# New numbers for the whole work order of a fused attention and feed-forward kernel, with a constant and a copy moved from VectorE to ScalarE

## The chip, the cores and the metric

The kernel runs on one core of a Trainium2 chip. Its engines are TensorE (PE in the profile, PEld for its weight loads), VectorE (DVE), ScalarE (ACT), GpSimd (POOL) and SyncE (SP), which here only issues DMAs. Each engine takes its own instructions strictly in the order in which they were built, and waits at the head of its queue for what other engines owe it. The metric is the device time of one execution in microseconds. Three executions took 1113.07, 1113.84 and 1115.66 us; the median is 1113.84 us. The profile is of one further execution, which took 1110.31 us and whose span from the first to the last instruction is 1108.5 us.

## The reference

Kernelised attention with random features, and behind it a feed-forward network with GELU:

```
scale = 1 / sqrt(sqrt(64));  q, k = q * scale, k * scale
phi(x) = exp(h - max(h)) / sqrt(128),  h = x @ omega.T - sum(x*x)/2
kv  = sum over s of phi(k)[s] outer v[s];   z = sum over s of phi(k)[s]
out = (phi(q) @ kv) / (phi(q) @ z + 1e-6)
x   = out, heads side by side              # 4608 tokens x 512
y   = gelu(x @ w_in) @ w_out               # w_in 512 x 2048, w_out 2048 x 512
```

There are 8 batches and 8 heads of 576 tokens with 64 dimensions, and 128 features.

## The kernel before

The attention is cut into 32 **units**, each with two heads of one batch. The first four (batch 0) are worked on in a plain form before the feed-forward starts; the next four (batch 1, `mode == 1`) in a middle form; the 24 units of batches 2 to 7 (`mode == 2`) in an exact split form, which is most of the work. The feed-forward runs over 12 **blocks** of 384 tokens. A block has 16 **chunks** of 128 hidden columns: `mm1` (L706, 12 matmuls of 384 columns), GELU and its two halves on ACT (L718, L719) and DVE (L724), and two chunks later `mm2` (L740 to L742, 9 matmuls of 512 columns). Block 0 is computed in fp32 (L693, L736), the other eleven in split fp16.

A unit of the third form goes through these steps:

- `x_high`, `x_low` (ACT L286, POOL L292): a slice of k or q is copied rounded and its rest subtracted, into one of three buffers `r`. `proj` (PE L299, 5 groups) and `proj_q` (PE L327, 4 groups) project it; `proj_lo` and `proj_add` (ACT L304, DVE L310, L311) take k's results, `q_blocks` (DVE L335, L337) q's. `k_shift` (POOL L316) subtracts k's maxima.
- `q_max` to `q_shift`: the maximum of q over all features. PE turns the partial maxima (L343), DVE reduces and spreads them (L347, L349), PE turns them back (L353), ACT copies (L356), DVE adds them to q's half of the tile `et` (L362). Then `exps` (ACT L370) takes all of `et`.
- `k_high`, `k_low`, `kv` (POOL L423, DVE L431, PE L450), five groups: the products with v. `kv_a` to `kv_d` (ACT L459, DVE L466 to L468, ACT L474, DVE L478) bring the sums into `kvh` and `kvl`: the numerators' columns, and beside them the denominator's column spread to 64 columns.
- `q_back`, `q_high`, `q_low`: q's exponentials in their layout.
- `num`, `den`, `div`, once for each half of the tokens: six matmuls (PE L518); two copies of the denominators (ACT L527, L528) into `dt`; then DVE turns `dt` (L535), adds the constant (L536), takes the reciprocal (L537), turns it back (L538) and multiplies (L546, L547) into `xs`, the input of a block. For the first two forms `den` is one copy (L525).

At the start of a block `block_max` (DVE L658), a short chain over PE, DVE and POOL (L192 to L215, L670 to L672), `block_high` and `block_low` (ACT L679, DVE L684) make the block's scales and its split input.

All results of PE's attention steps go into one ring of three PSUM banks, named `at`: a step that needs a bank waits until the step that had it has been read.

What sets the order is a list of **events**. Each step is entered with a number, its slot: `at(t, step, ...)`. The events are sorted by slot and the instructions are recorded in that sequence. A chunk takes 6 slots, a block 96; a third-form unit stands at a burst `t` (every 33.4 slots for the first eight, then every 36), its steps at fixed distances from `t`. The slots are no times: they only decide which instruction stands before which.

Of the kernel before, what the change touches and what calls it, by code (L numbers as in the profile page):

```python
# [19 lines left out]
P = 128  # L20
# [5 lines left out]
TOP = 13  # L26


@with_exitstack
def favor_attention_ffn(ctx: ExitStack, tc: tile.TileContext, qT, kT, v, omT, w_in, w_out, out):  # L30
# [430 lines left out]
    def kv_b(u):  # L461
# [6 lines left out]
        nc.vector.tensor_copy(kz[:, 1:3], kvs[:, :, D:D + 1].broadcast_to([P, 2, D]))  # L468
# [52 lines left out]
    def den(u, half):  # L521
        pe, po = u.pn[half]
        u.dt = sp.tile([P, HS], F32, tag="dt", name="dt", bufs=1)
        if u.mode < 2:
            nc.scalar.copy(u.dt, po[:, 0:HS])  # L525
            return
        nc.scalar.copy(u.dt[0:D], pe[D:P, 0:HS])  # L527
        nc.scalar.copy(u.dt[D:P], po[0:D, 0:HS])  # L528

    def div(u, half):  # L530
# [5 lines left out]
        nc.vector.tensor_scalar(rc, rv[:, :, 0], EPS * (1.0 if u.mode < 2 else KSC), None, op0=ALU.add)  # L536
        nc.vector.reciprocal(rc, rc)  # L537
# [232 lines left out]
    for i, u in enumerate(units[:NJ]):  # L770
        t = BASE + 9 * i
        at(t - 4, load_plain, u)
        for g in range(3):
            at(t + 2 * g, proj_plain, u, g)
        at(t + 6, kv_plain, u, ps_any)
        at(t + 7.3, kvz_plain, u, ps_any)
        for g in range(3):
            at(t + 7 + g, q_trans, u, g, ps_any)
            at(t + 7.5 + g, q_copy, u, g)
        for half in range(2):  # L780
            at(t + 11.2 + half, num, u, half, ps_any)
            at(t + 11.3 + half, den, u, half)
            at(t + 11.4 + half, div, u, half)

    at(BASE - 3, nc.vector.memset, ones, 1.0)
    for i in range(NF):
        pi, po = piece(True, i), piece(False, i)
        w_events(pi, BASE + 1 + 5 * i if i < WEARLY else SUB * i - 27, (-6, 0, 1, 2, 3))
        w_events(po, 5.5 * i, (-7, 0, 1, 2, 3))
        for pc, t in ((pi, 72 + 4.5 * i), (po, 91 + 4.5 * i)):  # L790
            at(t, w_high, pc)
            at(t + 1, w_low, pc)
    for win, t in ((1, 68), (0, 86.5)):
# [4 lines left out]
    bursts = [5 + 20.5 * k for k in range(NJ)]  # L798
    bursts += [112 + 33.4 * k if k < 8 else 346 + 36 * (k - 7) for k in range(len(units) - 2 * NJ)]
    load_at = -40  # L800
    for k, u in enumerate(units[NJ:]):
# [3 lines left out]
        if u.mode == 1:  # L805
            first = t - 13 + 3 * (k == 0)
            for i in range(3):
                at(first + (0, 6, 7.5)[i], proj_mid, u, i)
            load_at = first + 7.7
            at(t + 5.5, kv_plain, u, ps_at)  # L810
            at(t + 8, kvz_plain, u, ps_at)
            for g in range(3):
                at(t + 9 + 2 * g, q_trans, u, g)
                at(t + 9.6 + 2 * g, q_copy, u, g)
        else:
            pk, pq = [t - 27 + 1.75 * i for i in range(NK)], [t - 16 + 2 * i for i in range(4)]
            load_at = pq[-1] - 1.8
# [110 lines left out]
```

## Time and profile before

| | |
|---|---|
| median of three runs | 1113.84 us |
| profiled execution, its span | 1110.31 us, 1108.5 us |
| mean granted clock of TensorE | 0.988 |
| third-form units, exponentials (ACT L370) | from 205 us to 946 us |

The span falls into four stretches: up to about 55 us the plain units and the loads; up to 205 us the first block in fp32, the middle units and the conversion of the weights; up to 942 us the 24 third-form units beside the fp16 blocks; and after that feed-forward alone. A row of a waits view reads: engine, tile and line that waited, the releaser, the time in total, how often, and the longest.

### The profile page before, as it was taken

The numbers are of one execution on the slowest core, as the hardware profiler recorded it, in microseconds if no ns is written. First come the engines' busy times: TensorE is split into PE (matmuls) and PEld (weight loads), VectorE is DVE, ScalarE is ACT, GpSimd is POOL, SyncE is SP. The second block draws the span as 40 slices with busy tenths as digits, with TensorE's granted clock in tenths as the row PEclk, the third lists the DMA queues.
The fourth block names the chain that finished last, engine by engine and source line by source line (L and its number), as shares of the span: only waits on it lengthen the run. The fifth ranks groups of instructions, "written<-read, shape, count | busy, mean of one in ns | idle before, by whom it ended". The sixth has DMA issues, their size and how long they took to land.

```text
span 1108.5 us, 17209 instructions
## 1 busy us (share of the span) xinstructions
PE 1031.4 (93%) x5949; PEld 604.4 (55%) x5949; DVE 829.7 (75%) x1888; ACT 650.4 (59%) x1298; POOL 472.7 (43%) x606
## 2 busy tenths in 40 slices
PE   8988898999899999989799999989889999999998
PEld 6654454555455555555455555555555555555555
DVE  6989759988988888887887887997687798631312
ACT  7866454656566766656466666656656656533332
POOL 2224336545566644545654445655434555100000
PEclk9999999999999999999999999999999999999999
DMA  8565421211222112122221122222112220000000
GB/s 233 168 184 168 125 55 34 72 35 54 84 55 55 48 58 55 46 73 55 56 73 45 33 74 55 56 83 56 34 51 55 56 84 1 1 29 1 29 1 29
DMA packets 46279, 70.91 MB, mean 64 GB/s; under 512 B 13680, under 2 KB 22256, under 8 KB 46192
## 3 DMA queue, kind: packets, MB, share of 16 engines
q1 hardware_dynamic: 46192, 69.81, 22.1%
q8 instruction: 47, 0.77, 0.3%
q14 instruction: 40, 0.33, 0.1%
HBM read 60.36 MB, written 9.44 MB: 63 GB/s over the span
## 4 chain that ended last, share of the span: by engine, by line
PE 40%; DVE 31%; ACT 8%; issue 4%; POOL 4%; DMA 1%; POOLq 0%; DVEq 0%; ACTq 0%
PE h L706 17%; PE acc L742 5%; PE acc L741 5%; PE acc L740 5%; DVE gl L724 5%; DVE et L335 3%; DVE mx L337 2%; DVE ql L386 2%; DVE kl L431 2%; ACT gh L719 2%; ACT et L370 2%; DVE wil L170 1%; DVE rt L535 1%; PE at L450 1%; ACT g L718 1%
## 5 line engine op out<-in xcount | busy, mean ns | idle before, releaser
L706 PE MATMUL h<-xl,wih 128*128 128x384 f16 x704 | 230.8, 328 | 0.0
L706 PE MATMUL h<-xh,wih 128*128 128x384 f16 x704 | 230.7, 328 | 0.0
L706 PE MATMUL h<-xh,wil 128*128 128x384 f16 x704 | 230.3, 327 | 0.0
L724 DVE SCALAR_TENSOR_TENSOR gl<-g,bs,gh 128x384 f16<-128x384 f32 x176 | 127.2, 729 | 129.3 <-ACT gh L719 128.7
L292 POOL TENSOR_TENSOR r<-xt,r 64x256 fp32r<-64x256 f32 (+2 forms) x216 | 170.4, 798 | 105.3 <-ACT r L286 83.7
L740 PE MATMUL acc<-woh,gh 128*128 128x512 f16 x528 | 200.2, 379 | 1.8 <-DVE o L753 1.8
L741 PE MATMUL acc<-woh,gl 128*128 128x512 f16 x528 | 199.1, 377 | 0.0
L742 PE MATMUL acc<-wol,gh 128*128 128x512 f16 x528 | 199.0, 377 | 0.0
L718 ACT ACTIVATE g<-h,bs 128x384 f32<-128x384 f32 x176 | 101.7, 579 | 153.9 <-PE h L706 152.7
L706 PEld LDWEIGHTS <-wih 128*128 128x128 f16 x1408 | 134.3, 98 | 83.5 <-issue 0.6
L423 POOL TENSOR_SCALAR kh<-et 128x256 f16<-128x256 f32 (+1 forms) x120 | 50.8, 429 | 224.1 <-ACT et L370 141.3
L286 ACT CAST r<-xt 128x256 fp32r<-128x256 f32 (+2 forms) x216 | 87.4, 406 | 80.1 <-PE at L327 70.1
L719 ACT ACTIVATE gh<-g,bs 128x384 f16<-128x384 f32 x176 | 106.6, 614 | 2.8
L706 PEld LDWEIGHTS <-wil 128*128 128x128 f16 x704 | 69.1, 98 | 42.6 <-issue 0.7
L742 PEld LDWEIGHTS <-gh 128*128 128x128 f16 x544 | 53.4, 98 | 59.1 <-issue 0.8
L150 POOL TENSOR_TENSOR w<-w,raw 128x512 int32<-128x512 int32 x32 | 42.4, 1328 | 90.1 <-DVE w L146 52.5
L740 PEld LDWEIGHTS <-gh 128*128 128x128 f16 x544 | 53.2, 98 | 41.8 <-issue 0.6
L741 PEld LDWEIGHTS <-gl 128*128 128x128 f16 x544 | 53.5, 98 | 37.6 <-issue 2.6
L327 PE MATMUL at<-r,om 128*128 128x288 f32 x192 | 55.0, 368 | 20.4 <-DVE rc L537 10.0
L377 DVE STREAM_TRANSPOSE qt<-et 128x288 f32<-128x288 f32 x96 | 43.8, 465 | 37.1 <-ACT et L370 36.9
L299 PE MATMUL at<-om,r 128*128 128x256 f32 x216 | 63.6, 366 | 7.8 <-DVE kvz L467 7.7
L431 DVE SCALAR_TENSOR_TENSOR kl<-et,kh 128x256 f16<-128x256 f32 (+1 forms) x120 | 54.3, 465 | 15.6 <-POOL kh L423 14.5
(174 smaller groups left out, 2022.1 us busy)
## 6 DMA issues: line engine op xcount, KB each, us to landing
xt<-in_kT SPq DMA_DIRECT2D x56, 288.0 KB, 3.8
xt<-in_qT SPq DMA_DIRECT2D x56, 288.0 KB, 3.8
v<-in_v SPq DMA_DIRECT2D x32, 320.0 KB, 3.2
out_x<-o SPq DMA_DIRECT2D x35, 256.0 KB, 2.0
raw<-in_w_in SPq DMA_DIRECT2D x16, 512.0 KB, 4.5
raw<-in_w_out SPq DMA_DIRECT2D x16, 512.0 KB, 3.7
out_x<-o SPq DMA_DIRECT2D x2, 128.0 KB, 1.7
om<-in_omT SPq DMA_DIRECT2D x2, 32.0 KB, 2.2
```

The source lines that it names most:

```text
L286: nc.scalar.copy(u.r[i][:, 0:b - a], xf[:, a:b])
L292: nc.gpsimd.tensor_tensor(r, xf[D:, a:b], r, op=ALU.subtract)
L299: nc.tensor.matmul(u.pp[i][:, t], r[:, t * P:(t + 1) * P], om, start=True, stop=True)
L327: nc.tensor.matmul(ps[:, 0:HS], om[:, i], r, start=(i == 0), stop=(i == 1))
L431: nc.vector.scalar_tensor_tensor(kl[:, :n], es, KSC, kh[:, :n], op0=ALU.mult, op1=ALU.subtract)
L706: nc.tensor.matmul(h[:, 0:T], w, (xh, xh, xl)[k], start=(i == 0), stop=(i == 3 * NJ - 1))
L718: nc.scalar.activation(g, h[:, 0:T], AF.Gelu, scale=bsc[n][1][:, 3:4])
L719: nc.scalar.activation(gh, g, AF.Copy, scale=bsc[n][1][:, 4:5])
L724: nc.vector.scalar_tensor_tensor(gl, g, bsc[n][1][:, 4:5], gh, op0=ALU.mult, op1=ALU.subtract)
L740: nc.tensor.matmul(acc, gh[:, s], woh[:, c, c0:c1], start=(c == 0), stop=False)
L741: nc.tensor.matmul(acc, gl[:, s], woh[:, c, c0:c1], start=False, stop=False)
L742: nc.tensor.matmul(acc, gh[:, s], wol[:, c, c0:c1], start=False, stop=(c == NF - 1))
```

## The change

Three edits of the computation, and new numbers for the order. `kv_b`'s last instruction, the copy that spreads the denominator's column, goes from DVE to ACT. `den`'s copies become activations of the kind Copy that add the constant as a bias. `div` no longer adds it, and takes the reciprocal straight from the turned tile.

```
-        nc.vector.tensor_copy(kz[:, 1:3], kvs[:, :, D:D + 1].broadcast_to([P, 2, D]))
+        nc.scalar.copy(kz[:, 1:3], kvs[:, :, D:D + 1].broadcast_to([P, 2, D]))
...
-            nc.scalar.copy(u.dt, po[:, 0:HS])
+            nc.scalar.activation(u.dt, po[:, 0:HS], AF.Copy, bias=EPS)
...
-        nc.scalar.copy(u.dt[0:D], pe[D:P, 0:HS])
-        nc.scalar.copy(u.dt[D:P], po[0:D, 0:HS])
+        nc.scalar.activation(u.dt[0:D], pe[D:P, 0:HS], AF.Copy, bias=EPS * KSC)
+        nc.scalar.activation(u.dt[D:P], po[0:D, 0:HS], AF.Copy, bias=EPS * KSC)
...
-        nc.vector.tensor_scalar(rc, rv[:, :, 0], EPS * (1.0 if u.mode < 2 else KSC), None, op0=ALU.add)
-        nc.vector.reciprocal(rc, rc)
+        nc.vector.reciprocal(rc, rv[:, :, 0])
```

The slots come from a table `X`; of its some 70 numbers these belong to the steps that the prediction speaks of:

```
-            pk, pq = [t - 27 + 1.75 * i for i in range(NK)], [t - 16 + 2 * i for i in range(4)]
+            pk, pq = [t + X['pk'] + X['dk'] * i for i in range(NK)], [t + X['pq'] + X['dq'] * i for i in range(4)]
...
-            for d, f in ((1.5, q_max), (2, q_max2), (2.5, q_max3), (3, q_max4), (3.5, q_shift)):
-                at(pq[-1] + d, f, u)
+            for d, f in enumerate((q_max, q_max2, q_max3, q_max4, q_shift)):
+                at(pq[-1] + X['qm'] + X['dqm'] * d, f, u)
```

with `pk` -27, `dk` 1.68, `pq` -16, `dq` 2.67, `qm` 3.26, `dqm` 0.12. The products with v start at `t` + 2.57 instead of `t` + 4, the second half's numerators 4.27 slots behind the first's instead of 5. Bursts go from 112 + 33.4 per unit to 110.11 + 34.16, and from the eighth on they stand 3.2 slots later than before, 36 apart as before.

What this does to the queues is shown at three places of one unit, the one whose exponentials start at 780.07 us in the profile. In the changed file every line up to `div` stands 9 further down and those behind it 8 (L335 becomes L344, L724 becomes L732).

DVE in the first half's `div`, from the turn of `dt` on, before:

```order
L535 STREAM_TRANSPOSE rt<-dt 128x288
L536 TENSOR_SCALAR rc<-rt 128x9
L537 RECIPROCAL rc<-rc 128x9
L538 STREAM_TRANSPOSE rt<-rc 128x288
L335 STREAM_TRANSPOSE et<-at 128x288
L546 TENSOR_TENSOR xs_1_8787<-at,rt 64x288
L547 TENSOR_TENSOR xs_1_8787<-at,rt 64x288
```

and in the change:

```order
L544 STREAM_TRANSPOSE rt<-dt 128x288
L545 RECIPROCAL rc<-rt 128x9
L546 STREAM_TRANSPOSE rt<-rc 128x288
L554 TENSOR_TENSOR xs_1_8748<-at,rt 64x288
L555 TENSOR_TENSOR xs_1_8748<-at,rt 64x288
L344 STREAM_TRANSPOSE et<-at 128x288
```

The addition is gone, and the turn of a `q_blocks` has moved from inside the division to behind it.

DVE around the maximum of q, before: the second half's division, the last `q_blocks` (L335, L337) and `q_max2` (L347, L349) stand mixed.

```order
L335 STREAM_TRANSPOSE et<-at 128x288
L538 STREAM_TRANSPOSE rt<-rc 128x288
L337 TENSOR_REDUCE mx<-et 128x9
L546 TENSOR_TENSOR xs_1_8787<-at,rt 64x96
L547 TENSOR_TENSOR xs_1_8787<-at,rt 64x96
L546 TENSOR_TENSOR xs_1_8866<-at,rt 64x192
L547 TENSOR_TENSOR xs_1_8866<-at,rt 64x192
L347 TENSOR_REDUCE sm<-at 36x32
L658 TENSOR_REDUCE xm<-xs_1_8787 128x1
L349 COPY sm<-sm 36x96
L724 SCALAR_TENSOR_TENSOR gl<-g,bs,gh 128x384
L362 TENSOR_TENSOR et<-et,nq 128x1152
```

In the change the division is finished ahead of these rows:

```order
L344 STREAM_TRANSPOSE et<-at 128x288
L732 SCALAR_TENSOR_TENSOR gl<-g,bs,gh 128x384
L346 TENSOR_REDUCE mx<-et 128x9
L356 TENSOR_REDUCE sm<-at 36x32
L358 COPY sm<-sm 36x96
L732 SCALAR_TENSOR_TENSOR gl<-g,bs,gh 128x384
L371 TENSOR_TENSOR et<-et,nq 128x1152
```

The four multiplications and the block's maximum no longer stand between the last partial maximum and `q_max2`'s two instructions.

POOL at the products with v (`kh` is k's high part, `r` the next unit's slices, `vb` and `v` the parts of v), before:

```order
L423 TENSOR_SCALAR kh<-et 128x256 x4
L292 TENSOR_TENSOR r<-xt,r 64x256
L386 TENSOR_TENSOR ql<-qt,qh 128x288
L423 TENSOR_SCALAR kh<-et 128x128
L393 TENSOR_SCALAR vb<-v 128x10x64
```

and in the change:

```order
L432 TENSOR_SCALAR kh<-et 128x256 x4
L432 TENSOR_SCALAR kh<-et 128x128
L301 TENSOR_TENSOR r<-xt,r 64x256
L395 TENSOR_TENSOR ql<-qt,qh 128x288
L301 TENSOR_TENSOR r<-xt,r 64x128
L402 TENSOR_SCALAR vb<-v 128x10x64
```

All five high parts now stand in a row; the next unit's slice and `ql` come behind them.

On PE the same matmuls are issued, 5520 in the program in both. Between the last `proj_q` and `q_max` there stood 8 matmuls of `mm1` in this unit (1.3 us at 0.1625 us each); now 12 and the three of one `mm2` group stand there. Between `q_max` and `q_max3` stood 4 of `mm1` and 5 of `mm2`; now it is 3 of `mm2`.

102 lines of the change are left out of this document (55 added, 47 removed).

## The prediction

> **What bounds the kernel now.** I read the page's head and its chain of work that ended last, then the busy time by stretch, then PE's waits in the stretches where PE idles.
>
> ```profile
> PE 1031.4 (93%) x5949; PEld 604.4 (55%) x5949; DVE 829.7 (75%) x1888; ACT 650.4 (59%) x1298; POOL 472.7 (43%) x606
> ...
> PE 40%; DVE 31%; ACT 8%; issue 4%; POOL 4%; DMA 1%; POOLq 0%; DVEq 0%; ACTq 0%
> ```
>
> PE is the fullest engine, yet only 40% of the chain that ended last is its own work and 31% is DVE's: PE's in-order queue often stands at an instruction for which DVE is late. So the gain to be had is PE's idle time, and a row of work taken from another engine counts only where PE waits for it. Where does PE idle? The two stretches in the middle, with the busy time of PE, PEld, DVE, ACT and POOL:
>
> ```profile
> 55.00:205.00 150.00, 133.45 (x597) 72.22 (x598) 120.38 (x243) 80.73 (x135) 64.21 (x67) 0.95 0.38 109
> 205.00:942.00 737.00, 686.29 (x4028) 403.95 (x4027) 616.24 (x1431) 467.97 (x943) 388.53 (x505) 0.99 0.20 56
> ```
>
> PE idles 737.0 - 686.3 = 50.7 us from 205 to 942 us, the stretch of the 24 third-form units, and 16.6 us from 55 to 205 us. Ahead of them the loads, behind them feed-forward alone leave little to move. What ended PE's idle time from 205 to 942 us:
>
> ```profile
> PE at L327 <- DVE rc L537: 10.0, 4, 4.2
> PE at L299 <- DVE kvz L467: 7.7, 6, 1.9
> PE at L327 <- DVE et L335: 5.6, 12, 0.5
> PE at L450 <- DVE kl L431: 5.5, 15, 1.4
> PE at L518 <- DVE kvl L478: 3.2, 4, 1.4
> PE at L343 <- DVE mx L337: 2.5, 5, 1.0
> PE at L518 <- DVE xs L546: 2.3, 2, 1.2
> PE at L327 <- DVE et L310: 2.2, 3, 0.9
> PE acc L740 <- DVE o L753: 1.8, 1, 1.8
> PE at L518 <- ACT kvh L474: 1.8, 3, 0.9
> PE at L327 <- DVE mx L337: 1.5, 2, 1.0
> PE at L353 <- DVE sm L349: 1.5, 7, 0.2
> PE at L203 <- DVE ct L200: 1.1, 2, 0.5
> ```
>
> These thirteen rows hold 46.7 of the 50.7 us. No single step is to blame: `proj_q` (L327) has 19.3 us, `num` (L518) 7.3 us in these rows, `proj` (L299) 7.7 us, `kv` (L450) 5.5 us. Idle time understates a wait, because a matmul's row reaches over the start of the next one:
>
> ```profile
> L706 PE MATMUL h<-xh,wih 128*128 128x384 f16 x704 | 230.7, 328 | 0.0
> 748.41 1.95 PE h L706 x12
> ```
>
> One row is 328 ns long, but in the chain twelve start within 1.95 us, one in 162.5 ns. So each gap that shows hides about 0.165 us more.
>
> **The three small edits.** Their rows, the DVE instructions that go and the ACT copies that change:
>
> ```profile
> L536 DVE TENSOR_SCALAR rc<-rt 128x9 f32<-128x9 f32 x64 | 22.5, 351 | 0.9
> L468 DVE COPY kvz<-kvs 128x128 f32<-128x128 f32 x24 | 7.0, 293 | 0.0
> L527 ACT COPY dt<-at 64x288 f32<-64x288 f32 x48 | 19.0, 395 | 14.0 <-PE at L518 11.4 <-DVE et L335 1.6
> L610 ACT ACTIVATE et<-at,nm 128x128 f32<-128x128 f32 x26 | 7.7, 410 | 0.0
> L496 ACT COPY qh<-h 128x128 f32<-128x128 f32 x2 | 0.6, 291 | 0.0
> ```
>
> DVE loses 64 x 351 ns + 24 x 293 ns = 29.5 us of its 829.7. ACT gains 24 copies of 128x128, at 291 ns 7.0 us. What an activation with a constant costs over a copy no row shows; the nearest pair at one size is 410 against 291 ns, so 0.12 us more, for 112 instructions 13.3 us, between nothing and that. ACT then has 650.4 + 20 = 671 us, 61% of the span. None of this is PE's time. On the path `num`, `den`, `div`, which frees two PSUM banks, 0.35 us of DVE goes and, of the two `den` in a row, some 0.12 us of the second comes on top: 0.2 us shorter. From `kv` to `num` the copy no longer stands on DVE, 0.29 us. Those 29.5 us are therefore worth only what is counted in the waits below.
>
> The activation's table is no risk: the program has 58 table loads before and after. The Trainium skill, page "ScalarE: Activation LUTs", section "Rules for kernel authors", gives about 0.3 us per ACTIVATE and 0.83 ns an element, by which I estimate a `den` at 0.54 us instead of 0.395. By that page the second `den` would add 0.15 us rather than 0.12 to a path, and the sum below would be about 1 us smaller; no run here shows that activation yet.
>
> **The new order, term by term.** Each term is the idle time above less what I leave of it. PE's cover is counted from the order, 0.1625 us for a matmul of `mm1` and, by its 512 instead of 384 columns, 0.217 for one of `mm2`.
>
> (a) `proj_q`, 19.3 us. It needs its slice `r` and a bank that `q_blocks` has read. Before, PE came back to the same bank after 8 matmuls of `mm1`, 1.3 us, while the reading turn (L335) stood inside a division on DVE. Now the division is closed first, the groups stand 2.67 instead of 2 slots apart, and the bank is often one that `num` left 4.5 us of PE work earlier. I leave a quarter, 5: **-14 us**.
>
> (b) `proj`, 7.7 us, for the bank of `kv`, free when L467 has run. 3.4 us of matmuls stand between in both orders. L468 stood ahead of L467 and is gone, 0.29 us; but `q_low` (0.61 us) now often stands between L466 and L467. I leave 4.7: **-3 us**.
>
> (c) `kv`, 5.5 us for `kl`. PE work between `q_max3` and the first `kl` shrinks from 8.1 to 6.6 us in most units. That chain:
>
> ```profile
> L362 DVE TENSOR_TENSOR et<-et,nq 128x1152 f32<-128x1152 f32 x24 | 33.3, 1388 | 1.4 <-ACT nq L356 1.1
> L370 ACT ACTIVATE et<-et 128x2304 f32<-128x2304 f32 x28 | 59.5, 2124 | 5.7 <-DVE et L362 4.6
> L423 POOL TENSOR_SCALAR kh<-et 128x256 f16<-128x256 f32 (+1 forms) x120 | 50.8, 429 | 224.1 <-ACT et L370 141.3
> L431 DVE SCALAR_TENSOR_TENSOR kl<-et,kh 128x256 f16<-128x256 f32 (+1 forms) x120 | 54.3, 465 | 15.6 <-POOL kh L423 14.5
> ```
>
> sums to 1.39 + 2.12 + 0.43 + 0.47 = 4.4 us, with PE's own transpose, a small copy on ACT and the hand-overs some 5.3. It fits under 6.6 with 1.3 us to spare. The later groups lose the slice of 0.8 us (L292) that stood between two `kh` on POOL. I leave 2.5: **-3 us**.
>
> (d) `num`, with the rarer rows 8.1 us. `kv` to `num` grows from 4.85 to 5.5 us of matmuls in most units and its chain loses 0.29 us. Against that the halves move together, from 4.1 to 3.0 us; the second half needs a bank of the first. Its path loses the 0.2 us of above and, where the unit is like the one shown, the turn of `q_blocks` inside the division; the cover loses 1.1 us. So it is tight, and where a store or a block's step stands in the division it will wait. I leave 4: **-4 us**.
>
> (e) `q_max`, 2.5 us: 12 `mm1` and 3 `mm2` instead of 8 `mm1`, 2.6 against 1.3 us, and no multiplications in between. I leave 0.5: **-2 us**. `q_max3`, with the rarer rows 1.9 us: only 3 `mm2`, 0.65 us, cover two DVE instructions. Before, one row of L658 kept them apart, and L724 stood behind them:
>
> ```profile
> 777.08 0.28 DVE L347 TENSOR_REDUCE sm<-at 36x32 f32<-36x128 f32 x1
> ...
> 777.87 0.23 DVE L349 COPY sm<-sm 36x96 f32<-36x96 f32 x1
> 778.15 0.62 DVE L724 SCALAR_TENSOR_TENSOR gl<-g,bs,gh 128x384 f16<-128x384 f32 x1
> ```
>
> Alone they need 0.28 + 0.23 us, PE's transpose and three hand-overs, about 1 us against a cover of 0.77: some 0.2 us in nearly each of 24 units, 4.4 where 1.9 were, **+2.5 us**.
>
> (f) The blocks' chain (L196, L203), 1.7 us: three blocks come 3 us closer behind the last `num` that feeds them (3.8 us of PE work, before 6.8): **+1.5 us**. L740's wait stays.
>
> The loads of k and q are entered 3 slots closer ahead of their first reader, about 15 instead of 18, at some 0.9 us of this stretch a slot (36 slots, 32.5 us: eight units in the 260 us from 619.9 to 879.9). They take 3.8 us and stay hidden, at nothing:
>
> ```profile
> xt<-in_kT SPq DMA_DIRECT2D x56, 288.0 KB, 3.8
> ```
>
> Together -22 us. The thirteen rows count 66 gaps; if 45 close, each with 0.165 us that doesn't show, that is **-7 us**. From 55 to 205 us this row leads:
>
> ```profile
> PE at L489 <- DVE et L646: 7.8, 2, 4.3
> ```
>
> DVE is busy 120 of 150 us there, and the divisions of eight units, 16 x 0.35 us, lose 5.6 us; but the weights' work still stands ahead of L646. I take **-3 us**, between -8 and +6. For waits that an order doesn't show I add a quarter of the gain from 205 us on that isn't hidden, **+5 us**. Sum: -22 - 7 - 3 + 5 = **-27 us**: the span 1108.5 becomes 1081.5 us, its execution 1110.3 becomes 1083. The median of the runs stands 3.5 us above the profiled execution, and from it -27 gives **1087 us**.
>
> If all of (a) to (d) went and the early waits by half, it would be -40 - 10 - 8 and the two additions, about -54: 1060.
>
> **Rivals.** *The waits come back elsewhere.* For it: in a chain of in-order queues a wait that goes is often only handed on, and the margins in (c) and (d) are near 1 us. Half of the terms (a) to (d) then stay: -12 us, 1102.
>
> *All margins hold*: the additions of 5 us fall away and 13 of the 16 us that (a) to (d) leave, -45 us, 1069. Against it: the early stretch, where DVE stays at 80%.
>
> *Hidden anyway*: the order's gains and new waits cancel, about 1114.
>
> *POOL's queue becomes the bound, and the kernel slower.* The last `proj_q` needs a slice that POOL makes behind `kv`'s last `kh`, the parts of v, more slices and `k_shift`. In one unit, the last `kh`, the needed slice (the first of the two in its row) and the `proj_q`:
>
> ```profile
> 760.09 0.30 POOL L423 TENSOR_SCALAR kh<-et 128x128 f16<-128x128 f32 x1
> 771.51 1.49 POOL L292 TENSOR_TENSOR r<-xt,r 64x288 fp32r<-64x288 f32 x2
> 773.96 0.50 PE L327 MATMUL at<-r,om 128*128 128x288 f32 x2
> ...
> L292 POOL TENSOR_TENSOR r<-xt,r 64x256 fp32r<-64x256 f32 (+2 forms) x216 | 170.4, 798 | 105.3 <-ACT r L286 83.7 <-DVE gl L724 5.0 <-issue 4.3
> L386 POOL TENSOR_TENSOR ql<-qt,qh 128x288 fp32r<-128x288 f32 x24 | 20.2, 841 | 5.0 <-ACT qh L382 3.4 <-DMA xt<-in_kT 0.2
> ```
>
> The slice is ready at 772.26, 1.7 us before PE takes it. The new order puts a slice (0.80 us) and `ql` (0.84 us) more behind the last `kh`, and 1.3 us more of matmuls between `kv` and that `proj_q`: 1.7 - 1.64 + 1.3 = 1.4 us are left. From there it decides: with POOL 3 us later each of 24 units waits 1.6 us, and `q_max`, `exps` and the next `kh` slip with it, +38 us; after the gain of 27 that is +11, **1125**. For it: POOL would have to hold that pace in shorter units. Against it: POOL is busy only 389 of 737 us. DVE and POOL disturb each other already: L724 takes 0.62 us at 778.15 and 1.55 us here, beside POOL's L411:
>
> ```profile
> 766.06 1.35 POOL L411 TENSOR_TENSOR vb<-v,vb 128x640 bf16<-128x640 f32 x1
> 766.27 1.55 DVE L724 SCALAR_TENSOR_TENSOR gl<-g,bs,gh 128x384 f16<-128x384 f32 x1 [0.45 <-ACT gh L719]
> ```
>
> The Trainium skill, page "GPSIMD Engine Reference", section "Specifications", says that the two share their SBUF interfaces and contend when VectorE has two SBUF inputs; the trace agrees with those two rows.
>
> **Chances.** Forecast (1077 to 1099) 0.45; all margins hold 0.15; waits come back 0.18; no change 0.05; slower 0.17. A measurement of this kernel tells 0.2%, 2.2 us, from no change. Faster 0.78, same 0.05, slower 0.17. The range goes from 1062 to 1115 and leaves out most of the slower case and the end of the best.
>
> **What would show it.** Right: L327's waits near 5 us and L343's near none; DVE about 800 us; eight third-form units in some 250 us instead of 260; L353 waiting in every unit, for L349's successor. Wrong: waits of `proj_q` for POOL's `r` in each unit (the slower rival), `num`'s second half waiting over 0.5 us a unit, `kl` late at the first group, or the stretch from 55 to 205 us longer.

## The result, and the profile after

The change takes **1088.61 us** (median of 4 runs, 1086.80 to 1090.31) against 1113.66 us (4 runs) before: a ratio of 0.9772, with a 95% interval of 0.9751 to 0.9792. The profiled execution took 1090.31 us, the slowest of the four, with a span of 1088.5 us; before it was 1110.31 and 1108.5 us. So the medians differ by 25.1 us, the two spans by 20.0.

In the changed file `x_low` is L301, `proj` L308, `proj_add` L319 and L320, `k_shift` L325, `proj_q` L336, `q_blocks` L344, `q_max` L352, `q_max3` L362, `kv` L459, `kv_b` L475 to L477, `kv_d` L487, `q_low` L395, the parts of v L402 to L420, `num` L527, `div` L544 to L555, the store L761 and L762. The page's engines and the head of the chain that ended last:

```profile
PE 1025.7 (94%) x5949; PEld 600.0 (55%) x5949; DVE 822.4 (76%) x1800; ACT 648.8 (60%) x1322; POOL 475.0 (44%) x606
...
PE 41%; DVE 34%; ACT 6%; issue 4%; POOL 2%; DMA 1%; DVEq 0%; POOLq 0%; ACTq 0%
```

DVE has 88 instructions fewer, 64 additions and 24 copies that were 29.5 us before, yet its busy time fell only by 7.3 us. And the chain is still handed between PE and DVE. The same two stretches as before, again PE, PEld, DVE, ACT and POOL:

```profile
55.00:205.00 150.00, 134.58 (x632) 73.36 (x632) 129.83 (x246) 84.92 (x142) 66.84 (x68) 0.99 0.40 118
205.00:942.00 737.00, 698.81 (x4123) 410.70 (x4122) 612.64 (x1376) 476.04 (x982) 392.76 (x511) 1.00 0.20 55
```

PE's idle time from 205 to 942 us went from 50.7 to 38.2 us. What ended it:

```profile
PE at L308 <- DVE kvz L476: 8.0, 14, 0.8
PE at L527 <- DVE xs L554: 5.9, 9, 1.5
PE at L527 <- DVE et L344: 5.3, 1, 5.3
PE at L527 <- DVE et L319: 3.5, 6, 0.6
PE at L336 <- POOL r L301: 2.6, 6, 0.9
PE at L459 <- DVE kl L440: 1.8, 5, 0.6
PE at L352 <- DVE mx L346: 1.6, 3, 0.8
PE at L527 <- DVE kvl L487: 1.6, 3, 1.0
```

`proj_q`, which led before with 19.3 us, has 3.6 us with the rarer rows. `num` has doubled, from 8.1 to 16.3 us, a third of it one single wait of 5.3 us. The starts of `exps` on ACT cut the span into three parts. This table has them for every kernel; the ratios are against the kernel before in the same comparison. A kernel whose ratio stands below another's, with intervals that do not meet, is faster.

| kernel | ratio (95% interval) | first third-form `exps` | to the last | rest | span, us |
|---|---|---|---|---|---|
| before | 1 | 206.6 | 739.2 | 162.7 | 1108.5 |
| the change | 0.9772 (0.9751 to 0.9792) | 202.8 | 726.4 | 159.3 | 1088.5 |
| e1, edits alone | 0.9885 (0.9865 to 0.9905) | 201.0 | 735.8 | 161.8 | 1098.6 |
| e2, order alone | 1.0080 (1.0061 to 1.0099) | 209.4 | 749.6 | 159.3 | 1118.3 |
| f1, change without the copy's edit | 0.9814 (0.9799 to 0.9829) | 201.4 | 728.8 | 159.3 | 1089.5 |
| f2, change without the constant's edit | 1.0053 (1.0036 to 1.0070) | 208.1 | 747.9 | 159.3 | 1115.3 |
| g4, change with a reduction in `div` | 0.9887 (0.9869 to 0.9905) | 208.9 | 731.3 | 159.4 | 1099.6 |
| e7, edits, only the q slots new | 1.0080 (1.0059 to 1.0102) | 204.1 | 755.1 | 160.4 | 1119.6 |
| e4, change with `dnum` 5 | 0.9819 (0.9799 to 0.9839) | 199.8 | 728.8 | 159.6 | 1088.2 |
| e3, change, third `o`, nine `xs` | 0.9927 (0.9906 to 0.9948) | 218.6 | 725.1 | 159.0 | 1102.7 |
| f3, change, third `o`, two `g` | 0.9813 (0.9798 to 0.9828) | 209.7 | 721.5 | 159.0 | 1090.2 |
| f4, change, two `g` | 0.9857 (0.9840 to 0.9875) | 210.3 | 727.9 | 159.7 | 1097.9 |
| h3, change, v loaded from POOL's queue | 0.9768 (0.9752 to 0.9783) | 200.7 | 724.0 | 160.0 | 1084.7 |
| h6, h3 and `kv_b` from PSUM | 0.9710 (0.9693 to 0.9726) | 199.9 | 716.7 | 160.1 | 1076.7 |

The change's 20.0 us of span are 3.8 up to the 24 third-form units, 12.8 in them, and 3.4 behind, where the last unit stands later among the blocks.

A part of this is TensorE's granted clock. In each of these profiles it falls to a half for a few stretches of 3.4 us or a multiple of that. From the first third-form `exps` on, such a stretch begins during every wait of PE of 2.7 us or more, or at most 2.3 us behind its end, and also at some shorter ones. Before, `proj_q` waits 4.17 us for L537, up to 546.5 us. The row behind it (PE, PEld, DVE, ACT, POOL, then the clock, 0.50), and `mm1`'s matmuls in it, which start 0.32 us apart and not 0.1625:

```profile
546.90:550.30 3.40, 3.40 (x13) 2.32 (x13) 2.45 (x6) 2.16 (x5) 0.72 (x1) 0.50 0.31 87
547.17 0.53 PE L706 MATMUL h<-xh,wih 128*128 128x384 f16 x1
547.50 0.53 PE L706 MATMUL h<-xh,wil 128*128 128x384 f16 x1
547.82 0.53 PE L706 MATMUL h<-xl,wih 128*128 128x384 f16 x1
```

A stretch costs up to half its length. Between the first and the last third-form `exps` there are 10.2 us of them before and 6.8 in the change, one stretch at its wait of 5.3 us: at most 1.7 us of the 12.8, where PE's shown idle time fell by 13.0. Ahead of the first there are 17.1 and 10.2 us of them: up to 3.4 us of the 3.8, where the shown idle time fell by only 1.3.

### The profile page after: what moved, and what is told of

Same layout as the page of the kernel before. It is cut to its first block, busy times and chain, and to the rows that moved or that the text cites. A ratio compares the mean times of both kernels' runs of the same rounds, so it can differ in the third digit from the quotient of the medians.

```text
span 1088.5 us, 17164 instructions
## 1 busy us (share of the span) xinstructions
PE 1025.7 (94%) x5949; PEld 600.0 (55%) x5949; DVE 822.4 (76%) x1800; ACT 648.8 (60%) x1322; POOL 475.0 (44%) x606
## 4 chain that ended last, share of the span: by engine, by line
PE 41%; DVE 34%; ACT 6%; issue 4%; POOL 2%; DMA 1%; DVEq 0%; POOLq 0%; ACTq 0%
PE h L714 17%; DVE gl L732 5%; PE acc L748 5%; PE acc L749 5%; PE acc L750 5%; DVE kl L440 3%; DVE ql L395 3%; ACT et L379 3%; PE at L527 3%; DVE et L319 2%; DVE nm L320 2%; DVE qt L386 2%; PE at L336 2%; DVE wil L179 2%; DVE xl L692 2%
## 5 line engine op out<-in xcount | busy, mean ns | idle before, releaser
L301 POOL TENSOR_TENSOR r<-xt,r 64x256 fp32r<-64x256 f32 (+2 forms) x216 | 172.5, 807 | 92.1 <-ACT r L295 77.8
L732 DVE SCALAR_TENSOR_TENSOR gl<-g,bs,gh 128x384 f16<-128x384 f32 x176 | 126.8, 721 | 97.0 <-ACT gh L727 96.2
L295 ACT CAST r<-xt 128x256 fp32r<-128x256 f32 (+2 forms) x216 | 86.3, 405 | 31.6 <-PE at L336 20.2
L308 PE MATMUL at<-om,r 128*128 128x256 f32 x216 | 61.5, 357 | 8.5 <-DVE kvz L476 8.0
L379 ACT ACTIVATE et<-et 128x2304 f32<-128x2304 f32 x28 | 59.4, 2123 | 7.6 <-DVE et L371 6.8
```

The lines of the kernel that those rows point to most:

```text
L295: nc.scalar.copy(u.r[i][:, 0:b - a], xf[:, a:b])
L301: nc.gpsimd.tensor_tensor(r, xf[D:, a:b], r, op=ALU.subtract)
L379: nc.scalar.activation(et, et, AF.Exp)
L732: nc.vector.scalar_tensor_tensor(gl, g, bsc[n][1][:, 4:5], gh, op0=ALU.mult, op1=ALU.subtract)
```

## The experiments

In these files lines ahead of `div`'s end stand 7 (f3, f4: 8) above the change's, since the table has one line; h3 and h6 have the change's own numbers. So `proj` is L301, `proj_q` L329, `q_blocks` L337, `num` L520.

**Edits alone, order alone.** The prediction had the order as the cause and priced the edits "only in the waits". e1 has the numbers of before in the table and the three edits; e2 has the change's numbers and the computation of before.

> The three edits with the slots of before. Theory (the order holds nearly all of the gain): PE waits for DVE at the same places, each chain is 0.2 to 0.3 us shorter, so 0 to 5 us less than before, a ratio of 0.995 to 1.000, and PE's idle time from 205 to 942 us stays near 48 us. Rival (the edits relieve DVE, and that is a third or more of the gain): a ratio of 0.992 or less, and the waits of proj_q (L327 of before, 19.3 us) fall by 6 us or more.

> The new slots with the computation of before: the constant is added on DVE and the column is spread on DVE. Theory: 2 to 6 us slower than the change, a ratio to before of 0.979 to 0.983; proj_q's waits stay near 4 us, and num and proj, which already wait 16 and 8 us in the change, wait some 3 us more. Rival (the slots only fit together with the edits): a ratio of 0.988 or more, with a wait in every unit at num's second half.

Measured: the edits alone give 0.9885, 12.8 us off; the order alone is **slower** by 0.8%, 8.9 us; both together give 25.4 us. So 21.5 us of the gain belong to neither alone, and the theory that the order carries nearly all of it falls. In e1 the rival's ratio is met, but not its other sign: `proj_q`'s waits fall by 2.7 us and not by 6, and PE idles 48.3 us from 205 to 942 us, as the theory had it. Of the 9.9 us by which e1's span is shorter, 5.6 lie ahead of the third-form units. PE's waits in e2, from 205 to 942 us:

```profile
PE at L520 <- DVE et L337: 13.0, 12, 2.0
PE at L520 <- DVE xs L548: 8.5, 8, 2.1
PE at L520 <- DVE et L312: 6.1, 9, 0.8
```

The new order does take `proj_q`'s waits away here too, but hands them to `num`, whose second half stands 4.27 slots behind the first and needs what the first half's division frees. In e1 `proj_q` still waits 16.6 us, 15.4 of them in these rows:

```profile
PE at L329 <- DVE xs L547: 5.8, 12, 0.9
PE at L329 <- DVE et L337: 5.8, 3, 2.8
PE at L329 <- DVE et L312: 3.8, 2, 1.9
```

**Which edit.** Each of the two undone by itself in the change:

```
f1:
-        nc.scalar.copy(kz[:, 1:3], kvs[:, :, D:D + 1].broadcast_to([P, 2, D]))
+        nc.vector.tensor_copy(kz[:, 1:3], kvs[:, :, D:D + 1].broadcast_to([P, 2, D]))
f2:
-            nc.scalar.activation(u.dt, po[:, 0:HS], AF.Copy, bias=EPS)
+            nc.scalar.copy(u.dt, po[:, 0:HS])
...
-        nc.scalar.activation(u.dt[0:D], pe[D:P, 0:HS], AF.Copy, bias=EPS * KSC)
-        nc.scalar.activation(u.dt[D:P], po[0:D, 0:HS], AF.Copy, bias=EPS * KSC)
+        nc.scalar.copy(u.dt[0:D], pe[D:P, 0:HS])
+        nc.scalar.copy(u.dt[D:P], po[0:D, 0:HS])
...
-        nc.vector.reciprocal(rc, rv[:, :, 0])
+        nc.vector.tensor_scalar(rc, rv[:, :, 0], EPS * (1.0 if u.mode < 2 else KSC), None, op0=ALU.add)
+        nc.vector.reciprocal(rc, rc)
```

> The changed kernel with one of its edits undone: kv_b's copy of the denominators' columns stands on VectorE again, as before the change; the constant stays in ScalarE's activations, the new slots stay. TensorE's order is that of the changed kernel instruction for instruction. Theory (what the edits are worth together with the new slots is that no other work enters a division: before's slots with the edits gave 1098.7 us, the new slots without them 1120.5, both together 1088.6): this edit doesn't touch the divisions, so it stays at 1087 to 1093 us, num's second halves wait for the multiplications and for q_blocks' turn some 16 us as in the change, and only the wait of num for kvz (kv_b and kv_c stand behind each other on VectorE again) grows, by at most 12 x 0.3 us. Rival (it is the copy that makes the new slots fit, by VectorE's queue behind kv_b): 1105 us or more, with q_blocks or kvz ahead of num at 25 us and more.

> The changed kernel with the other edit undone: ScalarE only copies the denominators, and VectorE adds the constant in an instruction of its own between the division's transposition and its reciprocal, as before the change; kv_b's copy stays on ScalarE, the new slots stay. Theory (the constant's instruction is what lets q_blocks' turn in: with it q_blocks stands inside a division at 71 places of the built order, in the changed kernel at 46, and what stands inside holds num's next half up): 1114 to 1122 us, near the new slots with neither edit (1120.5), with num waiting 25 us or more for q_blocks and the multiplications between 205 and 942 us, and a steady period of eight units of 261 us or more (254.6 in the change, 262.7 with neither edit). Rival (48 instructions of about 0.2 us on VectorE are all there is to it): 1089 to 1099 us, and the same waits as in the change. Rival two (only both edits together help): also 1114 or more, but then the kernel with the copy on VectorE alone is slow too.

Measured: 1092.45 and 1118.49 us. In ratios the copy is worth 0.0042, 4.7 us, though the two spans differ by 1.0 us only, and the constant 0.0281, **31 us**: 64 instructions of 128x9. But what the expectation offered as the reason, other work that gets into the division, was only a count in the built orders (71 instructions of `q_blocks` inside the 48 third-form divisions against 46). The trace has another candidate.

**What the constant's instruction waits for.** The row of all 64 in f2: shortest, median and longest in ns.

```profile
L538 DVE TENSOR_SCALAR rc<-rt x64: 130/174/1860, 20.1 to 977.2; 128x9 f32<-128x9 f32 x64
```

Half of them take 174 ns or less, and the longest ten times that. One of the long ones in f2's timeline, DVE and POOL together:

```profile
349.22 0.43 DVE L537 STREAM_TRANSPOSE rt<-dt 128x288 f32<-128x288 f32 x1
...
349.63 2.11 POOL L318 TENSOR_TENSOR et<-et,nm 128x1152 f32<-128x1152 f32 x1
349.91 1.86 DVE L538 TENSOR_SCALAR rc<-rt 128x9 f32<-128x9 f32 x1
351.80 0.22 DVE L539 RECIPROCAL rc<-rc 128x9 f32<-128x9 f32 x1
```

POOL's two-operand subtraction ends at 351.74; the small addition, which began behind it, ends at 351.77. In f2 all 14 that last 0.8 us or more end 0.02 to 0.04 us behind a two-operand instruction of POOL, ten times `k_shift`, as here, and four times another. It is a wait, but the trace books it as busy time of DVE and no waits view shows it. It was there before the change:

```profile
412.85 2.11 POOL L316 TENSOR_TENSOR et<-et,nm 128x1152 f32<-128x1152 f32 x1
413.09 0.47 DVE L535 STREAM_TRANSPOSE rt<-dt 128x288 f32<-128x288 f32 x1
413.59 1.40 DVE L536 TENSOR_SCALAR rc<-rt 128x9 f32<-128x9 f32 x1
```

In the 48 third-form divisions the time over 174 ns sums to 10.3 us before, 18.3 us in f2 and 19.6 us in e2: with the new slots it lasts 0.8 us or more 13 times instead of 7, in f2 ten times beside `k_shift`, before all seven. The turn (L535) beside the same instruction of POOL keeps its length, 0.47 us. The Trainium skill, page "SBUF — State Buffer", section "Who interferes with whom", says that VectorE and GpSimd share a pair of ports as an exclusive lock, that the one that starts first blocks the other to its end, and that `tensor_scalar` can take the pair while `tensor_reduce` never does. By that page a reduction in the addition's place would not be held; the next run is that case.

g4 is the change with such an instruction more, a maximum over one element, which leaves the value as it is. VectorE's sequence is f2's but for this instruction, and TensorE's is nearly f2's.

```
         nc.vector.transpose(rt, u.dt)
-        nc.vector.reciprocal(rc, rv[:, :, 0])
+        nc.vector.tensor_reduce(rc, rv[:, :, 0:1], axis=AX.X, op=ALU.max)
+        nc.vector.reciprocal(rc, rc)
```

> The changed kernel with one more small VectorE instruction in each division, between the transposition and the reciprocal, where the constant's instruction stood: a maximum over one element (TENSOR_REDUCE 128x9), which changes no value. Against the kernel without the constant's edit (1118.5 us) VectorE's and TensorE's instructions come in nearly the same sequence, 71 steps of q_blocks inside the divisions as there; only the form at the constant's place is another. In that kernel's trace the constant's TENSOR_SCALAR lasts 0.17 us as a rule, but 19 of 48 times 0.4 to 1.86 us or so, and then it ends within 0.05 us of the end of a two-input instruction of POOL (19.7 us over its median in all); reciprocals, reductions and transpositions are never seen to last longer. Theory A (the constant's instruction is held by POOL's instruction, inside the division): the reduction lasts 0.15 us each time, and the time falls to 1089 to 1100 us, with num's waits for q_blocks at 5 us or less. Theory B (an instruction more lets q_blocks' turn into the division, and that order is what costs): 1113 to 1120 us, with the waits of the kernel without the edit (12 us for q_blocks, 7.5 for the multiplications). A third outcome, 1101 to 1112 us, is some of both.

Measured: 1100.42 us, 0.4 us above theory A's bound. (Of the 48 additions in f2, 15 last 0.4 us or more by the trace, not 19.) The row and the same place of g4's timeline, where POOL's instruction runs until 350.25:

```profile
L538 DVE TENSOR_REDUCE rc<-rt x64: 122/158/173, 20.4 to 961.5; 128x9 f32<-128x9 f32 x64
```

```profile
348.14 2.11 POOL L318 TENSOR_TENSOR et<-et,nm 128x1152 f32<-128x1152 f32 x1
348.41 0.15 DVE L538 TENSOR_REDUCE rc<-rt 128x9 f32<-128x9 f32 x1
348.59 0.22 DVE L539 RECIPROCAL rc<-rc 128x9 f32<-128x9 f32 x1
```

No reduction is held; the rule that the Trainium skill's page gives agrees. `num`'s wait for `q_blocks` halves against f2, 6.2 instead of 12.2 us, though not to the 5 that theory A set; its wait for the multiplications goes from 7.5 to 4.7:

```profile
PE at L520 <- DVE et L337: 6.2, 7, 3.8
PE at L520 <- DVE xs L548: 4.7, 6, 1.6
```

So of the 31 us some 18 (0.0166 of ratio) are the hold: 16.6 of the 26.8 us between the spans of f2 and the change lie in the 24 units between f2 and g4. The other part comes with the reduction too, which is not held: 4.9 us in the units and 6.1 us ahead of them. Both kernels have `q_blocks` inside the divisions 71 times, the change 46 times, but that this is the price isn't shown: e7 below has them there only 21 times and is as slow as e2. All kernels that keep the early buffers and have an instruction there begin the third-form units at 206.6 to 209.4 us, and those without at 199.8 to 204.1. Sixteen divisions of the first two forms lie there. The clock has a share in it: up to the first third-form `exps` it is at a half for 13.7 to 17.1 us in the former, and for 3.4 to 10.2 in the latter. Which waits bring that about was not followed further.

**The q groups' slots alone.** e7 has the edits, the numbers of before, and only the five numbers of the q groups new (`pq`, `dq`, `qb`, `qm`, `dqm`).

> The slots of before, but for the five that place the q groups (pq, dq, qb, qm, dqm), which are those of the change; all three edits. With before's slots and the edits the time was 1098.7 us, and proj_q's waits 15 us between 205 and 942 us for q_blocks and the multiplications. Theory (the order's share of the gain, 10 us, comes from the q groups, whose second turn in each division no longer stands ahead of the multiplications): 1089 to 1094 us, proj_q's waits at 5 us or less, num's at 10 us or less. Rival (the pitch of the q groups only hands the wait on, and the other slots had to move with it): 1096 us or more, with num's waits for q_blocks or for the multiplications up by what proj_q's fell.

Measured: 1122.79 us, 0.8% slower than before and, by the ratios, 22 us slower than e1, which lacks these five numbers. The theory falls: `proj_q`'s waits went from 16.6 to 8.5 us, and `proj`'s wait for `proj_add`, 6.5 us in e1, became the longest.

```profile
PE at L301 <- DVE et L312: 20.7, 15, 1.7
PE at L452 <- DVE kl L433: 6.1, 11, 1.2
PE at L329 <- DVE rc L538: 6.1, 2, 3.0
```

The wait was handed on, as the rival said, though most of it to `proj`; `num`'s waits rose too, from 6.0 to 12.9 us, but for `kvl` and `kvh` and not for `q_blocks` or the multiplications. So these five are worth nothing without others of the table; which others, no run shows.

**The distance of `num`'s halves.** e4 puts `dnum` back from 4.27 to 5.

> The change with num's second half 5 slots behind the first, as before, instead of 4.27. Theory (the halves were moved too close, so num waits for the first half's bank): the waits of num for xs, 5.9 us in the change, fall below 3 us, and the time by 2 to 4 us, to about 1085. Rival (the place further back only delays the banks that proj_q and q_max take next): num's waits fall, but those of proj_q or q_max rise by as much, and the time is within 2 us of the change or above it.

Measured: 1091.23 us, by the ratios 5 us slower than the change, though the profiled span is the same within 0.3 us; in any case no gain. `num`'s wait for the multiplications goes, and `proj_q` has it instead:

```profile
PE at L329 <- DVE xs L547: 8.5, 12, 1.5
```

**The single wait of 5.3 us.** In the change's timeline, POOL's, SP's and DVE's rows at the second half of one `num`:

```profile
369.17 0.80 DVE L761 TENSOR_SCALAR o<-acc,bs,wsc 128x512 f32<-128x512 f32 x1
...
370.30 1.54 POOL L420 TENSOR_TENSOR vb<-v,vb 128x640 bf16<-128x640 f32 x1
...
371.87 0.33 SPq L283 DMA_DIRECT2D v<-in_v  x1
372.25 3.09 SPq L762 DMA_DIRECT2D out_x<-o  x2
372.35 0.20 DVE L545 RECIPROCAL rc<-rt 128x9 f32<-128x9 f32 x1
...
377.45 0.81 DVE L761 TENSOR_SCALAR o<-acc,bs,wsc 128x512 f32<-128x512 f32 x1 [4.90 <-DMA out_x<-o]
378.18 0.47 DVE L546 STREAM_TRANSPOSE rt<-rc 128x288 f32<-128x288 f32 x1
378.29 0.33 SPq L762 DMA_DIRECT2D out_x<-o  x1
```

A load of v waits on SP until POOL has read the v before it (L420, to 371.84). The stores of finished rows stand behind it, so neither of the two buffers `o` comes free, and the scaling that wants one stands inside a division. The first store's row was written by 369.97 us, and the store was issued at 372.25, 2.3 us later. It then took until 377.35 to land, 5.1 us where the median of its line is 2.0; no run parts these two shares of the wait. Four kernels go after it: a third `o`, with room from two `xs` (e3) or from one `g` and a moved constant tile (f3; f4 is the same without the third `o`), or v loaded from POOL's own queue (h3):

```
-        nc.sync.dma_start(u.v[:, :, 0:D], v[u.b, u.j])
+        (nc.gpsimd if u.mode == 2 else nc.sync).dma_start(u.v[:, :, 0:D], v[u.b, u.j])
```

> The change with three instead of two buffers for the stored rows (o), and 9 instead of 11 for the blocks' input to make room. In the change one store waits 4.9 us on DVE for an earlier store's transfer, which stands on SP behind a load of v that waits for POOL; the division around it stands too, and num's second half waits 5.3 us. Theory (that is one wait and all of its price): it goes, some 5 us less than the change, about 1083 us, and no wait of num is over 2 us. Rival (PE catches up elsewhere, the wait is handed on to q_max and the next exponentials): less than 2 us gained.

> The changed kernel with a third buffer for the output row o of the blocks' store, so that the scaling that writes o no longer waits for a store that stands on SP's queue behind a load of v that itself waits for POOL. The room for it comes from the activations g (two buffers in place of three) and from om32, which moves into a pool of the early stretch; the number of xs buffers is left alone, so the early work stays in its order (the first third-form exps at 203 us, where the version with nine xs buffers had 218.6). Theory (the one-off 5.3 us is SP's queue order): the wait of num at 374 to 379 us goes, the stretch between the exps at 356 and 390 us is 28 to 29 us and not 34.5, and the time is 1082 to 1085 us, 0.994 to 0.997 of the change. Rival (the missing third g buffer costs as much: mm1's GELU waits for mm2 to release g): 1088 us or more, with L714 or the activation of g waiting for mm2 in the trace, and the control with two g buffers alone slower than the change by as much.

> Control to the kernel with three o buffers: the changed kernel with two g buffers and om32 in the early pool, and two o buffers as before. If g's third buffer is idle: 1087 to 1091 us, and the 5.3-us wait of num behind the store stands as in the change. If it is needed: slower by the price that the kernel with three o buffers pays too, 1093 us or more.

> The changed kernel, in which the loads of v of the third-form units are issued by POOL's queue in place of SP's. A load of v waits until POOL has read v's last use, and on SP's queue the stores of the blocks stand behind that wait; on POOL's own queue nothing of SP stands behind it. TensorE's and VectorE's instructions come in the same sequence as in the change, and no buffer changes. Theory (the 5.3-us wait at 374 to 379 us is a store held up on SP's queue by a load of v): the scaling of o there waits under 1 us, the stretch between the exps at 356 and 390 us is 28 to 29 us, not 34.5, and the time is 1082 to 1085 us. Rival (issuing a load occupies POOL, or POOL's queue brings v later): POOL's busy time or its waits grow, v_a starts later and kv waits for vb; 1088 us or more.

Measured: the stretch between the two `exps` around it is 34.5 us in the change, 28.3 in e3, 28.3 in f3, 34.1 in f4 and 28.8 in h3. So the cause is shown to be the store behind the load, and it costs 5.7 to 6.2 us there. That holds the stretch at half clock too, from 376.2 to 383.0 us in the change, which e3, f3 and h3 don't have at this place. Each remedy pays some of that back. Two `xs` fewer delay the first third-form `exps` by 15.8 us, the room taken in f3 and f4 by 7 us; the third `o` itself is worth 0.0044, 4.9 us, of f3 against f4. In h3 the store goes out in time:

```profile
370.58 0.20 DVE L545 RECIPROCAL rc<-rt 128x9 f32<-128x9 f32 x1
370.70 0.75 DVE L761 TENSOR_SCALAR o<-acc,bs,wsc 128x512 f32<-128x512 f32 x1
```

But eight later units take 256.4 us instead of the change's 254.6. An issue takes 0.6 us of POOL, 24 times, and `proj_q`'s wait for POOL's `r` grows from 2.6 to 3.7 us; that this is all of it isn't shown. Its 1086.99 us can't be told from the change.

**A held instruction on PE's path.** With the wait booked as busy time, other two-operand rows can be read anew. The longest row of PE's waits above ends with `kvz`, made by `kv_b`'s second addition (L476); the first (L475) makes what it reads. Their rows in the change, and `kv_d`'s and `q_low`'s:

```profile
L395 DVE TENSOR_TENSOR ql<-qt,qh 128x288 fp32r<-128x288 f32 x72 | 48.0, 667 | 0.9 <-ACT qh L391 0.9
L475 DVE TENSOR_TENSOR kvs<-kvs 128x128 f32<-128x128 f32 x24 | 20.2, 840 | 0.3
L487 DVE TENSOR_TENSOR kvl<-kvz,kvh 128x256 fp32r<-128x256 f32 x24 | 20.1, 836 | 1.3 <-ACT kvh L483 1.3
L476 DVE TENSOR_TENSOR kvz<-at,kvs 128x128 f32<-128x128 f32 x24 | 6.7, 281 | 1.2
```

L475 and L476 are of one shape; L476 reads one operand from PSUM. h6 is h3 and this edit, which takes the second operand from the PSUM bank, and not from ScalarE's copy of the same numbers:

```
-        nc.vector.tensor_tensor(kvs[:, :, 0:D], kvs[:, :, 0:D], kvs[:, :, D + 1:VW - D], op=ALU.add)
+        nc.vector.tensor_tensor(kvs[:, :, 0:D], kvs[:, :, 0:D], u.pkv[:, :, 2 * D + 1:VW], op=ALU.add)
```

> The kernel with the loads of v on POOL's queue, and one more edit that changes no value: the first addition of kv_b takes its second operand from the PSUM bank, in place of ScalarE's copy of it. As a two-operand instruction on SBUF alone (kvs<-kvs, 128x128) it lasts 0.27 us at the least, but 0.80 us in the median and up to 1.45 us in the change, 20.2 us for 24; VectorE's two-operand instructions with an operand in PSUM are never seen to last longer than others of their shape (the next line, kvz<-at,kvs of the same shape: 0.24 to 0.29 us). TensorE's sequence stays that of the change; kvz, which it makes, ends 14 waits of proj, 8.1 us. Theory (instructions on SBUF are held by POOL's two-operand instructions, those with PSUM are not): all 24 last 0.3 us or less, VectorE's busy time falls by 13 us, proj's waits for kvz fall from 8 to 2 to 4 us, and the time goes 3 to 7 us under the kernel with v on POOL alone (1087.0): 1080 to 1084 us. Rival one (the hold is not of the operand's place): the instruction lasts 0.8 us in the median as before and the time stays at 1087. Rival two (the hold goes, but ScalarE's copy of kvz or POOL is late next): the instruction lasts 0.3 us, and the time stays within 2 us of 1087, with num's wait for kvl or proj's for POOL in the place of kvz's.

Measured: **1079.95 us**, a ratio of 0.971, the fastest of all. The row, and what is left of the wait:

```profile
L475 DVE TENSOR_TENSOR kvs<-kvs,at 128x128 f32<-128x128 f32 x24 | 6.6, 274 | 0.3
```

```profile
PE at L336 <- POOL r L301: 6.1, 8, 1.2
PE at L527 <- DVE xs L554: 5.0, 7, 1.6
...
PE at L308 <- DVE kvz L476: 1.3, 6, 0.3
```

840 became 274 ns, `proj`'s wait 8.1 (h3) became 1.3 us, and POOL's slice `r` is late more often, 6.1 instead of 3.7 us. The time fell by 7.0 us against h3 (by the ratios 6.5), the upper end of the expectation, and lies below the change's with intervals that do not meet. The clock has no share in this: h3 and h6 have no stretch at half clock from the first third-form `exps` on. The rule of the Trainium skill's page "SBUF — State Buffer" agrees again: it counts an instruction with two operands in SBUF among those that contend, and one with a single operand there not.

## Why the prediction was right, and where it was not

The forecast of 1087 us stands 1.6 us from the median, and that is in part luck. The sum was made for the profiled executions, -27 us, and these differ by 20.0. The other 5 us are where the two executions lie among their runs: the one before 3.4 us under its median, the change's 1.7 above. Its parts, shown waits from 205 to 942 us:

| step | predicted | measured |
|---|---|---|
| (a) `proj_q` | -14 | -15.7 (19.3 to 3.6) |
| (b) `proj` | -3 | +0.3 (7.7 to 8.0) |
| (c) `kv` | -3 | -3.3 (5.5 to 2.2) |
| (d) `num` | -4 | **+8.2** (8.1 to 16.3) |
| (e) `q_max`, `q_max3` | -2, +2.5 | -0.9, -0.4 |
| (f) the blocks' chain | +1.5 | +0.4 |
| not shown | -7 | about 0 |
| up to the first third-form `exps` | -3 | -3.8 |
| waits not foreseen | +5 | counted in (b) and (d) |
| behind the last unit | 0 | -3.4 |

Shown idle fell by 12.5 us and the stretch between the first and the last `exps` by 12.8, so by this account the hidden -7 isn't there. What doesn't show as idle time is the clock, at most 1.7 us of it. From 205 us on the sum had -24 us in the units; the runs gave about half of that. The -3 up to the first `exps` came as -3.8, but not as the divisions' loss on DVE: L646's 7.8 us of wait became 6.2, all of PE's idle time there fell by 1.3, and up to 3.4 us are the clock. The 3.4 us behind the last unit stood in no term.

**Step (d) failed.** It named a second half that waits over 0.5 us a unit as a sign of being wrong, and `num` waits 16.3 us in 24 units. The step took the path of `num`, `den`, `div` as 0.2 us shorter and the halves' cover as just enough. 5.3 us of its 16.3 are the store behind SP's queue: step (d) named a store in the division as a risk, but not SP, whose queue the prediction looked at only for k's and q's loads. Another 5.9 us are the multiplications, which e4 moves back to `proj_q`: the pitch of the halves and `proj_q`'s bank share one budget, and (a) and (d) were counted as if apart.

**The three small edits were mis-sized, and the cause was misplaced.** "On the path 0.35 us of DVE goes", "worth only what is counted in the waits": 351 ns was the mean of instructions of 174 ns in the median and some of up to 1395, held by POOL. On the path such a one costs the hold, not the mean. The row of the mean hides that; the shortest, median and longest of the line would have shown it. Without this edit the new order is slower than the old (f2, e2). The prediction quoted a held row, L724 beside L411, and a page of the Trainium skill on it, and kept it for the rival. The step in (a), "now the division is closed first", has the same fault: of the instructions of `q_blocks` 82 stood inside the 48 divisions before, 71 with the change's slots and the addition kept, 46 in the change. Most of it is the addition's doing, not the slots'. `div` records its instructions in one piece, and yet others stand inside it in the trace: the order that is built is not the order of the slots, and the description of the events as a plain recorded sequence is too simple. By what rule the builder moves them no run shows.

**DVE "about 800 us"** came out as 822.4: the additions and copies went, but `kvs` rose from 12.7 to 20.2 us, `kvl` from 15.1 to 20.1 and `ql` from 43.1 to 48.0, the same numbers of instructions of the same shapes. All that last 0.25 us more than the shortest of their row end at a fixed distance behind an instruction of POOL: 0.14 to 0.15 us for `kvs`, 0.27 to 0.28 for `kvl`, 0.30 to 0.32 for `ql`. Of `kvl` these are 17 of 24 in the change, 8 before, of `ql` 24 of 72, 12 before; those of `kvs` are held for longer. For `kvs` h6 shows that the hold goes with the place of one operand. So (b) stayed where it was: the copy L468, which stood ahead of `kvz` in 21 of 24 units, went with its 0.29 us, and the addition ahead of `kvz` grew from 0.53 to 0.84.

**The activation with a constant** costs 0.01 us, not 0.12. The two rows of `den` in the change, 395 ns before:

```profile
L536 ACT ACTIVATE dt<-at 64x288 f32<-64x288 f32 x48 | 19.6, 408 | 50.7 <-PE at L527 37.0 <-DVE et L344 6.3 <-DVE xs L555 5.8
L537 ACT ACTIVATE dt<-at 64x288 f32<-64x288 f32 x48 | 19.3, 402 | 9.3 <-PE at L527 8.1
```

The 0.3 us that the prediction took from the Trainium skill's page "ScalarE: Activation LUTs" are there for a bias given by a pointer. For one given as an immediate, as here, its section "What ACT_TABLE_LOAD costs" has 186 ns and 0.833 ns an element, an estimate of 426 ns, and the 402 and 408 ns measured come near that.

**The rivals.** POOL as the bound did not come: `proj_q` waits 2.6 us in all for `r`. Waits that come back elsewhere did, and in the rival's size: the shown waits of (a) to (d) fell by 10.5 us, where the forecast had 24 and the rival half of that. The median comes near the forecast nevertheless, by the 3.4 us behind the units and the 5 us of the executions. *All margins hold* and *hidden anyway* did not come: (d) rose, and the units did take 12.8 us less. Of the signs, eight units came at 254.6 us, between the 250 that would show it and the 260 of before, and L353's successor (L362) waits only twice, 1.5 us in all, not in every unit.

## What to carry to other kernels

Look at the shortest, median and longest of a small VectorE instruction before taking its mean: where the longest end together with a GpSimd instruction, the busy time is a wait, and a form that reads PSUM, a reduction, or another engine takes it off the path. Don't add up waits that one budget holds together: e2, e4 and e7 each move a wait to a neighbour that takes banks from the same ring. Look at the granted clock around a long wait of TensorE: here those of 2.7 us and more brought a stretch at half clock with them. Read every in-order queue that a step is on, a DMA issuer's too, for what stands ahead of it and waits.

## What the runs showed of the hardware

- A VectorE addition of 128x9 takes 0.17 us, and up to 1.86 us when a GpSimd instruction with two operands in SBUF began before it; it then ends 0.02 to 0.04 us behind that one (f2). The same hold is seen on two-operand instructions with both in SBUF (`kvs` 128x128 in the change: 0.27 to 1.45 us), beside GpSimd instructions with one operand too. It is not seen on the reduction of 128x9 (at most 0.17 us, g4), the reciprocal (0.22 us), the transposition of 128x288 (0.48 us), nor with one operand in PSUM (0.25 to 0.29 us for `kvs` in h6).
- A DMA that waits on SP's queue holds up what stands behind it: a store whose row was written at 369.97 us was issued at 372.25, right behind a load of v that had waited for GpSimd.
- TensorE's granted clock goes to a half for 3.4 us or a multiple of that during or behind waits of 2.7 us and more; `mm1`'s matmuls then start 0.32 us apart and not 0.1625.
- A load of v issued from GpSimd's queue takes 0.58 to 0.75 us of that engine.
